# A new written-out order for the opening of a one-core attention and MLP kernel, with nine more constant matmuls and some evictions on other engines

## The chip, the cores and the metric

The kernel runs on one core of a Trainium2 chip. The metric is the device time in microseconds (us), the median of several runs; a profiled execution of the same program gives the trace. A core has five engines that run side by side: TensorE (PE in the profile; its weight loads are PEld), VectorE (DVE), ScalarE (ACT), GpSimd (POOL) and SyncE (SP). In this kernel SP issues all DMA transfers, from one queue.

## The reference

All inputs are float32; x is 1 x 2048 x 512.

```
xn = layernorm(x)                                # over the 512 columns, no affine part
qkv = xn @ wqkv                                  # 32 heads of 16
logits[s, w] = q[s] . k[s - 2w] / 4   for w = 0..7   (masked where s - 2w < 0)
s  = (softmax(logits) applied to v[s - 2w]) @ wo
y  = layernorm(xn)
h  = gelu(y @ w1 + b1)                           # 512 -> 1376
g  = silu(h @ w2 + b2)                           # 1376 -> 512
out = x + s * g
```

## The kernel before

**Numbers.** Every large matmul is done in three float16 passes: each float32 operand is split into a high half (rounded) and a low half (what the rounding left), and TensorE adds high x high, low x high and high x low in PSUM. So every activation tile and every weight block has two steps of preparation, "hi" (a scaled copy or a cast) and "lo" (a subtraction), and each is given to an engine by a table of constants at the top of the file.

**Tiles.** The sequence is split in even and odd positions (c = 0 and 1), 1024 rows each, 8 tiles of 128 rows. The heads are taken in 4 head blocks of 8 heads; a head block's weight is 512 x 384 (q, k and v). There are 8 units of attention (c, head block). Each unit has a projection on TensorE (12 matmuls of 384 columns a tile, L864), evictions of PSUM into the buffer U with a row scale (L878 on VectorE, L882 on ScalarE), halo copies of k and v by DMA (L896), products and sums on VectorE (L930, L933, L988) and GpSimd (L999, L1010), a split of the result (L971 ScalarE, L973 VectorE) and its transposition by DMA (L976). The MLP runs beside it on TensorE in 4 chunks of 4 tiles (L1143 first matrix, L1186 second). At the end the output projection is done for c = 1 (L1088), with the last head block's part in separate matmuls that come "late", after the last transposition.

**The opening.** SP loads, in an order given by the constant `LOADS` and by `ORDER` below: tiles of x as they are ("x"), two tiles already transposed on the host ("t", tiles 6 and 7), halves of the first two head blocks' weights ("q": q 0 is k = 0, 1 of the first block, q 2 is k = 2, 3; q 4 and q 6 are the second block), the four parts of the MLP's first matrix ("w"), a bias ("b"). Then:

- Tiles 6 and 7 go a direct way: their mean over columns is formed (tile 6: L685 on VectorE and a small matmul L691; tile 7: four matmuls L682), subtracted (L693, VectorE), and they are multiplied in float32 with the unscaled head block (L700, four steps a tile, step k needs quarter k of the head block).
- The first head block is scaled: squares summed on ScalarE (L597), added up over partitions by tiny matmuls (L513), a power of two worked out on VectorE (L524 to L542), then four "hi" copies on ScalarE (L619) and four "lo" steps, two on VectorE (L626) and two on GpSimd (L553, L554).
- Every x tile has statistics on VectorE (L659, L660, L714), a power on GpSimd (L718), a normalisation (L748 GpSimd, L744 ScalarE, L751 VectorE, by `Y_ENG`), and is transposed: tiles 0 to 3 by TensorE (L766), followed by a cast "hi" (L770 ScalarE or L772 VectorE, by `HI_ENG`) and a subtraction "lo" (L773); tiles 4 to 7 by a cast, a subtraction and a DMA (L756 to L758).
- The projection of the first two head blocks is issued in groups of four matmuls, so that the first four can start as soon as "hi" of a tile and of the weights are there.
- `WAKE` constant matmuls (L1305; 128 x 128 by 256 columns of constants, result unused) are issued on TensorE around the first steps.

**What sets the order.** The kernel first builds a list of operations (`Plan.add`): each has an engine, what it reads and writes, and a number in the order in which it was added. `Plan.issue` then emits them. `ORDER` (L73) lists all numbers, so the order of every engine's queue, SP's too, is written out and nothing is chosen at build time; costs and priorities in the code no longer matter. Buffers of a ring are handed out in that order too. Each engine works through its queue in order; between engines there are semaphores. An operation that is not ready therefore holds up all that stand behind it on its engine.

Of the kernel before, what the change touches and what calls it, by code (L numbers as in the profile page):

```python
# [10 lines left out]
BF16 = mybir.dt.bfloat16  # L11
# [7 lines left out]
P = 128  # L19
S, D, F = 2048, 512, 1376  # L20
H, DH, W, DIL = 32, 16, 8, 2
KT = D // P
# [10 lines left out]
LASTP = 256  # L33
# [19 lines left out]
HI_ENG = ('act', 'act', 'act', 'dve', 'dve', 'dve', 'dve', 'act')  # L53
XT = (0, 4, 30, 34)
# [7 lines left out]
EV0 = ('act', 'dve', 'dve', 'act', 'act', 'act', 'dve', 'dve')  # L62
EV1 = ('dve', 'dve', 'act', 'act', 'act', 'act', 'dve', 'act')
# [5 lines left out]
W2LATE = 6  # L69

# [287 lines left out]
PW1 = 0.423  # L358
PB1 = 0.75
PCS = 0.6  # L360
PQ0 = 0.2677
PSQ0 = 0.1788
PMEAN = 0.04
PDIR = (0.192, 0.1517, 0.1187, 0.1556)
# [1162 lines left out]
```

## Time and profile before

| | us |
|---|---|
| median of 3 runs | 412.66 |
| lowest, highest run | 412.56, 412.87 |
| span of the profiled execution | 411.0 |
| TensorE busy | 402.8 |
| VectorE busy | 381.6 |
| ScalarE busy | 224.9 |
| GpSimd busy | 132.7 |

The span is from the first to the last instruction of one execution; the run's time has something more around it. A row of a timeline has the start, the duration, the engine, the line of the program, the operation with its output and input and how many instructions were merged (x16), and in brackets how long the engine was idle before and what ended that. Consecutive rows can overlap a little, because an instruction's end is drawn with its pipeline. A float32 matmul of L682, L691 and L700 is recorded as two instructions.

### The profile page before, as it was taken

The numbers are of one execution on the slowest core, as the hardware profiler recorded it, in microseconds if no ns is written. First come the engines' busy times: TensorE is split into PE (matmuls) and PEld (weight loads), VectorE is DVE, ScalarE is ACT, GpSimd is POOL, SyncE is SP. The second block draws the span as 40 slices with busy tenths as digits, with TensorE's granted clock in tenths as the row PEclk, the third lists the DMA queues.
The fourth block names the chain that finished last, engine by engine and source line by source line (L and its number), as shares of the span: only waits on it lengthen the run. The fifth ranks groups of instructions, "written<-read, shape, count | busy, mean of one in ns | idle before, by whom it ended". The sixth has DMA issues, their size and how long they took to land.

```text
span 411.0 us, 5490 instructions
## 1 busy us (share of the span) xinstructions
PE 402.8 (98%) x2030; PEld 198.7 (48%) x2030; DVE 381.6 (93%) x386; ACT 224.9 (55%) x372; POOL 132.7 (32%) x141
## 2 busy tenths in 40 slices
PE   7899999999999999999999999999999999999996
PEld 4565544444444455445544554444445544444443
DVE  4899999999999999999889999899999989989985
ACT  3899987983989736633564164214523177236310
POOL 2843000053562425143424243233322505250012
PEclk9999999999999999999999999999999999999999
DMA  8957538251018372911251009610344452004984
GB/s 288 395 104 227 177 90 214 92 179 27 1 30 189 85 130 77 150 49 27 51 141 27 0 2 213 209 50 22 107 122 120 107 135 60 0 1 116 285 214 162
DMA packets 52627, 48.04 MB, mean 117 GB/s; under 512 B 37066, under 2 KB 37510, under 8 KB 52088
## 3 DMA queue, kind: packets, MB, share of 16 engines
q1 hardware_dynamic: 52600, 47.69, 42.8%
q8 instruction: 16, 0.26, 0.3%
q14 instruction: 11, 0.09, 0.1%
HBM read 24.40 MB, written 7.34 MB: 77 GB/s over the span
## 4 chain that ended last, share of the span: by engine, by line
PE 90%; DVE 3%; ACT 3%; DMA 1%; POOL 1%; issue 0%; SPq 0%; POOLq 0%; ACTq 0%; DVEq 0%
PE ps L864 27%; PE z L1186 25%; PE ps L1143 25%; PE ps L1056 5%; PE z L1088 2%; PE ps L1088 2%; PE z L1174 2%; DMA prod<-in_A_x_dram 1%; DVE bn L659 1%; ACT w L565 1%; ACT w L504 1%; PE pl L1088 1%; PE z L1177 1%; PE pl L864 1%; POOL prod L748 1%; DVE yT L773 0%
## 5 line engine op out<-in xcount | busy, mean ns | idle before, releaser
L864 PE MATMUL ps<-wq,yT 128*128 128x384 f16 (+1 forms) x708 | 128.9, 337 | 0.2
L1186 PE MATMUL z<-w,h 128*128 128x512 f16 x480 | 111.4, 379 | 0.0
L1143 PE MATMUL ps<-yT,w 128*128 128x512 f16 x480 | 109.0, 379 | 0.0
L864 PEld LDWEIGHTS <-yT 128*128 128x128 f16 x744 | 72.2, 98 | 59.1 <-issue 1.3
L930 DVE TENSOR_TENSOR prod<-U 128x2048 f32<-128x2048 f32 x32 | 73.8, 2312 | 4.1 <-ACT U L882 3.0
L1143 PEld LDWEIGHTS <-w 128*128 128x128 f16 x480 | 46.8, 98 | 55.6 <-issue 0.5
L933 DVE TENSOR_REDUCE L<-prod 128x128 f32<-128x2048 f32 x32 | 73.0, 2282 | 0.5
L1186 PEld LDWEIGHTS <-h 128*128 128x128 f16 x480 | 46.5, 98 | 54.6 <-issue 0.7
L999 POOL TENSOR_TENSOR prod<-prod,prod 128x1024 f32<-128x1024 f32 x14 | 41.3, 2968 | 81.3 <-DVE prod L988 81.3
L882 ACT ACTIVATE U<-ps,cs 128x384 f32<-128x384 f32 x54 | 30.1, 575 | 62.9 <-PE ps L864 62.7
L988 DVE TENSOR_TENSOR prod<-pl,U 128x2048 f32<-128x2048 f32 x28 | 63.5, 2283 | 0.3
L1156 ACT ACTIVATE ps<-ps,b1T,hsc 128x512 f32<-128x512 f32 x40 | 29.8, 747 | 37.0 <-PE ps L1143 36.8
L1159 ACT ACTIVATE h<-ps,hsc 128x512 f16<-128x512 f32 x40 | 27.4, 684 | 20.6 <-PE z L1186 19.7
L1009 POOL COPY gate<-prod 1x1 f32<-1x1 f32 x21 | 4.6, 219 | 102.2 <-DVE prod L930 102.2
L1010 POOL TENSOR_TENSOR prod<-prod 128x1024 f32<-128x1024 f32 x14 | 32.9, 2348 | 0.0
L1161 DVE SCALAR_TENSOR_TENSOR h<-ps,hsc,h 128x512 f16<-128x512 f32 x40 | 29.5, 744 | 3.2 <-ACT h L1159 3.2
L1056 PE MATMUL ps<-wo,oT 128*128 128x512 f16 x96 | 21.5, 379 | 0.0
L983 DVE TENSOR_TENSOR prod<-prod,prod 128x2048 f32<-128x2048 f32 x9 | 20.6, 2288 | 0.2
L971 ACT ACTIVATE o<-prod,osc 128x1024 f16<-128x1024 f32 (+1 forms) x9 | 9.5, 1051 | 18.0 <-DVE prod L983 9.9
L1010 POOL TENSOR_TENSOR prod<-prod,prod 128x1024 f32<-128x1024 f32 x7 | 16.4, 2347 | 0.0
L1088 PEld LDWEIGHTS <-oT 128*128 128x128 f16 x108 | 10.5, 98 | 10.4 <-issue 0.2
L1056 PEld LDWEIGHTS <-oT 128*128 128x128 f16 x96 | 9.4, 98 | 11.1
(201 smaller groups left out, 393.6 us busy)
## 6 DMA issues: line engine op xcount, KB each, us to landing
f<-in_A_x_dram SPq DMA_DIRECT2D x31, 256.0 KB, 3.1
U<-U SPq DMA_DIRECT2D x16, 392.0 KB, 6.7
gd<-f SPq DMA_DIRECT2D x12, 256.0 KB, 2.7
prod<-in_A_x_dram SPq DMA_DIRECT2D x8, 256.0 KB, 5.7
oT<-in_B_w_dram SPq DMA_DIRECT2D x2, 1024.0 KB
yT<-in_B_w_dram SPq DMA_DIRECT2D x2, 1024.0 KB
f<-gd SPq DMA_DIRECT2D x8, 256.0 KB, 5.4
out_dram<-f SPq DMA_DIRECT2D x8, 256.0 KB
```

Source lines behind the costliest of these rows:

```text
L864: nc.tensor.matmul(b.t[:, 0:wide], y[:, s, k, o:o + P], wq[hb][:, t, k], start=(n == 0), stop=(n == 11))
L882: act(384, lambda i=i, b=b: nc.scalar.activation(U3[:, i:i + 31:15, :], b.t[:, 0:384].rearrange("p (t e) -> p t e", t=3), AF.Identity, sca ...
L930: dve(2048, lambda p2=p2, g=g: nc.vector.tensor_tensor(p2(), q, slots(Ut, KH, 2 * g), op=ALU.mult), qk + [("kh", ub, 0), ("kh", ub, 1), (" ...
L933: dve(2048, lambda pr=pr, g=g: nc.vector.tensor_reduce(L3()[:, 2 * g:2 * g + 2], pr.t.rearrange("p (r f d) -> p r f d", r=2, d=DH), AX.X, ...
L988: dve(2048, lambda: nc.vector.tensor_tensor(pr.t.rearrange("p (r f d) -> p r f d", r=2, d=DH), A3()[:, 2 * g:2 * g + 2].rearrange("p r (f ...
L999: pool(2.4, lambda n=n: nc.gpsimd.tensor_tensor(acc.t[:, n:n + 1024], acc.t[:, n:n + 1024], p1.t[:, n:n + 1024], op=ALU.add), [acc, p1], [ ...
L1010: nc.gpsimd.tensor_tensor(x.t[:, 0:1024], x.t[:, 0:1024], y(), op=ALU.add)
L1056: nc.tensor.matmul(b.t, oT[:, hb, i // 4, s, i % 4], wo[:, t, hb], start=(hb == 0 and n == 0), stop=(hb == last and n == 2))
L1088: nc.tensor.matmul(b.t[:, cols], oT[:, hb, i // 4, s, i % 4], wo[:, t, hb, cols], start=(start and hb == 0 and n == 0), stop=(stop and hb ...
L1143: nc.tensor.matmul(b.t[0:M], w1[:, s, f * 512 + k * M:f * 512 + (k + 1) * M], yT[ch][:, t, k], start=(n == 0), stop=(n == 11))
L1156: act(512, lambda: nc.scalar.activation(b.t[0:M], b.t[0:M], AF.Gelu_apprx_tanh, bias=b1T[0:M, f:f + 1], scale=hsc[0:M, 1:2]), [b, ("b1T",) ...
L1186: nc.tensor.matmul(z.t, hl[s][:, t * P:(t + 1) * P], w2[:, w, f], start=(f == 0 and n == 0), stop=False)
```

## The change

Three things change what is emitted; the rest of the diff adds choices that are all set to what the kernel did before (`SUBS`, `ST_ENG`, `YLO`, `SECS`, `QH0`, `QH1`, `LASTC`, more entries in `XT` and `PDIR`, a new branch of `MEANBY`) or costs that only a planner without `ORDER` would read.

**Engines.** In the first head block's evictions, tiles 1 and 2 go from VectorE to ScalarE and tiles 3 and 4 the other way; in the second's, tiles 0 and 6 go to ScalarE and tile 2 to VectorE. The cast of tile 3 goes to ScalarE. The "hi" of the weight piece W1P[5] (1024 columns) goes from ScalarE to VectorE.

**Constant matmuls.** 28 instead of 19. The first 19 stand ahead of tile 6's mean matmul (before: 16), 4 behind it, and 5 are strewn over the queue: behind tile 7's mean, behind tile 0's transposes, two behind the second group of projections of tile 0 and one behind the last of the second block's totals.

**ORDER.** It is a new list, 1273 numbers instead of 1264, and nearly all queues differ from beginning to end. What the first operations are, queue by queue:

| queue | before | after |
|---|---|---|
| SP | t6, q0, q2, x2, x0, q4, t7, x5, x1, x3, x4, q6, w0, w2, x7, w3, x6, w1, b | t6, q2, q0, x0, t7, x2, x1, q4, x4, x5, x3, q6, w3, w2, w1, x7, x6, b, w0 |
| TensorE (without constants) | mean 6, direct 6 k=0, 1, two totals, k=2, mean 7, k=3, total, transposes 0, direct 7 (four), transposes 1, total, projection 0 (4, 4), transposes 3, projection 1 (4), 3 (4, 4, 4), ... | mean 6, direct 6 k=0, two totals, k=1, mean 7, k=2, direct 7 k=0, 1, transposes 0, direct 6 k=3, direct 7 k=2, projection 0 (4), total, direct 7 k=3, projection 0 (4), total, transposes 3, 1, 2, projection 3 (4), 1 (4), 3 (4), 1 (4, 4), 3 (4), ... |
| VectorE | mean 6, subtract 6, statistics 2, 0, scale of block 0, statistics 5, subtract 7, statistics 1, lo of weights, lo of tile 0, statistics 4, 3, ... | mean 6, subtract 6, statistics 0, scale of block 0, statistics 2, subtract 7, statistics 1, 4, 5, 3, lo of tile 0, ..., normalise 3, 2, lo of weights, scale of block 1, lo of weights, lo of tiles 3, 1, ... |
| ScalarE | squares q0, q2, q4, four hi of weights, cast 0, squares q6, normalise 1, ... | squares q2, q0, three hi of weights, squares q4, cast 0, fourth hi, squares q6, normalise 1, normalise 4, cast 3, cast 1, ... |
| GpSimd | power 0, normalise 0, power (1, 2), lo of weights, power (3, 4, 5), power of second variance, lo of weights, normalise 5, ... | power 0, normalise 0, lo of weights, power (1, 2), power (3, 4, 5), power of second variance, lo of weights, ..., normalise 5 |

Further on: VectorE's eviction of the second head block's tile 2 stands behind evictions and casts and ahead of weight halves and the first attention product (L930), and at the end two steps of the output (L1120, L1127) stand ahead of the last split (L973), which came before them.

The core of the diff:

```
-HI_ENG = ('act', 'act', 'act', 'dve', 'dve', 'dve', 'dve', 'act')
+HI_ENG = ('act', 'act', 'act', 'act', 'dve', 'dve', 'dve', 'act')
-W1ENG = ('act', 'dve', 'act', 'act', 'act', 'act', 'act')
+W1ENG = ('act', 'dve', 'act', 'act', 'act', 'dve', 'act')
-EV0 = ('act', 'dve', 'dve', 'act', 'act', 'act', 'dve', 'dve')
-EV1 = ('dve', 'dve', 'act', 'act', 'act', 'act', 'dve', 'act')
+EV0 = ('act', 'act', 'act', 'dve', 'dve', 'act', 'dve', 'dve')
+EV1 = ('act', 'dve', 'dve', 'act', 'act', 'act', 'act', 'act')
 ORDER = (
-    0, 1, 235, 19, 2, 3, 4, 5, 6, 7, 8, 9, 10, 11, 110, 111, 112, 113, 114, 115, 116, 117, 118, 119, 120, 121,
-    122, 123, 124, 125, 20, 126, 127, 128, 21, 32, 33, 163, 22, 23, 34, 54, 37, 12, 109, 108, 38, 40, 49, 35,
...
+    110, 244, 0, 109, 2, 1, 111, 112, 113, 108, 4, 114, 6, 115, 116, 117, 118, 119, 120, 121, 122, 33, 123, 124,
+    125, 3, 129, 8, 19, 134, 131, 20, 130, 32, 127, 128, 21, 135, 22, 37, 38, 34, 35, 40, 23, 36, 54, 5, 26, 49,
...
-WAKE = 19
+WAKE = 28
```

More of the change, by code (lines that the diff above doesn't have):

```diff
@@ L32 @@
 NFB = 7
-LASTP = 256
+LASTC = (0, 256, 512)
 LASTPOOL = (0, 2, 4)
@@ L69 @@
 W2LATE = 6
+SUBS = ()
+ST_ENG = ('dve',) * 8
+YLO = ('dve',) * 8
+SECS = BATCHES
+QH0 = ('act', 'act', 'act', 'act')
+QH1 = ('act', 'act')
 BEFORE_W1 = (0, 1, 4, 5)
 ORDER = (
[62 rows of a table removed]
[62 rows of a table added]
 )
@@ L671, in tile_mixer, with parts, xcs @@
     xt = {i: U[1][:, XT[n] * P:(XT[n] + 4) * P].rearrange("p (k t) -> p k t", k=KT) for n, i in enumerate(FP)}
+    def parts(i):
+        return ((0, 1), (1, KT)) if i in SUBS else ((0, KT),)
+    def xcs(i):
+        return [("xc", i, k0) for k0, k1 in parts(i)]
     def center(i):
@@ L706, in tile_mixer, with stats_act @@
     gof = {i: g for g in GROUPS for i in g}
+    def stats_act(i):
+        q, (x, xkey) = cpos[i], xk[i]
+        sm = R_s.new()
+        o, dst = (i % 4) * P, yT[i // 4]
+        junk = dst[:, 0, :, o:o + P].bitcast(BF16)
+        act(512, lambda: nc.scalar.activation(x(), x(), AF.Identity, accum_out=sm.t[:, 0:1]), [xkey], [xkey, (sm, 0)], aps=2)
+        act(1, lambda: nc.scalar.activation(mv0[:, q, 0:1], sm.t[:, 0:1], AF.Identity, scale=1.0 / D), [(sm, 0)], [("mv0", i)])
+        act(1, lambda: nc.scalar.activation(sm.t[:, 1:2], sm.t[:, 0:1], AF.Identity, scale=-D ** -1.5), [(sm, 0)], [(sm, 1)])
+        act(512, lambda: nc.scalar.activation(
+            junk, x().rearrange("p (k t) -> p k t", k=KT), AF.Square, bias=sm.t[:, 1:2], scale=D ** -0.5,
+            accum_out=mv0[:, q, 1:2]), [xkey, (sm, 1), ("mv0", i)], [("mv0", i), ("yh", 0, i)], aps=3)
     def ln0(g):
@@ L851, in qkv @@
         cp = lambda i: cpos[i] if c == 0 else i
-        raw = pl.users([("xc", j) for j in FP]) if u == 1 else set()
+        raw = pl.users([x for j in FP for x in xcs(j)]) if u == 1 else set()
         wide = 384 + FL * (hb == HLAST)
@@ L1090, in mm @@
             return go
-        parts = [(i, slice(0, D)) for i in range(NI - 1)] + [(NI - 1, slice(0, LASTP)), (NI - 1, slice(LASTP, D))]
+        parts = [(i, slice(0, D)) for i in range(NI - 1)] + [(NI - 1, slice(a, b)) for a, b in zip(LASTC, LASTC[1:])]
         banks = {}
@@ L1291, in tile_mixer @@
                     y0(i)
-    for n, g in enumerate(BATCHES):
+    for n, g in enumerate(SECS):
         with prio(PSEC[n]):
```

43 lines of the change are left out of this document (31 added, 12 removed), and 120 rows, old and new, of the table ORDER.

## The prediction

> **What bounds the kernel now.** I read the page first, then a table of stretches, then the timelines of the opening and of the end.
>
> ```profile
> span 411.0 us, 5490 instructions
> PE 402.8 (98%) x2030; PEld 198.7 (48%) x2030; DVE 381.6 (93%) x386; ACT 224.9 (55%) x372; POOL 132.7 (32%) x141
> PE 90%; DVE 3%; ACT 3%; DMA 1%; POOL 1%; issue 0%; SPq 0%; POOLq 0%; ACTq 0%; DVEq 0%
> ```
>
> TensorE is busy 98% and carries 90% of the chain that ended last; VectorE with 93% stands close behind it. The table of stretches says where TensorE's missing share lies (in each row, the second figure is TensorE's busy time, the fourth VectorE's):
>
> ```profile
> 0.00:5.00 5.00, 3.81 (x17) 2.70 (x18) 1.51 (x5) 1.74 (x2) 2.59 (x11) 1.00 0.64 209
> 5.00:10.00 5.00, 3.42 (x13) 1.64 (x12) 2.75 (x9) 2.00 (x5) 0.19 (x1) 1.00 1.02 360
> 10.00:15.00 5.00, 4.20 (x21) 2.93 (x22) 4.25 (x12) 4.04 (x11) 4.06 (x4) 1.00 1.03 408
> 15.00:20.00 5.00, 4.42 (x26) 2.37 (x25) 4.45 (x18) 4.22 (x7) 4.39 (x6) 1.00 1.03 405
> 20.00:60.00 40.00, 39.87 (x228) 21.81 (x226) 38.21 (x64) 37.30 (x67) 8.29 (x6) 1.00 0.54 145
> 60.00:300.00 240.00, 239.91 (x1200) 116.15 (x1199) 229.71 (x198) 134.76 (x231) 86.96 (x86) 1.00 0.37 91
> 300.00:396.00 96.00, 96.00 (x475) 45.56 (x474) 90.79 (x70) 40.52 (x55) 22.06 (x28) 1.00 0.43 114
> 396.00:411.00 15.00, 11.17 (x60) 5.57 (x57) 9.91 (x16) 0.32 (x1) 4.18 (x3) 1.00 0.55 176
> ```
>
> In the first 20 us TensorE idles 1.19 + 1.58 + 0.80 + 0.58 = 4.15 us. From 20 to 396 it idles 0.13 + 0.09 + 0 = 0.22 us in all. So the time is: when TensorE gets going, plus a fixed amount of matmul, plus the tail. Only the opening has time to give, and an order that is worse later can only take. The opening as TensorE lives it:
>
> ```profile
> 1.19 3.57 PE L1305 MATMUL z<-first,fours 128*128 128x256 bf16 x16 [1.19 <-DVE first L440]
> 4.64 0.79 PE L691 MATMUL ps<-f,first 128*128 128x128 f32 x2
> 6.21 1.56 PE L700 MATMUL pl<-prod,U 128*128 128x384 f32 x4 [0.27 <-DVE U L693]
> 10.12 1.16 PE L682 MATMUL ps<-U,first 128*128 128x128 f32 x8 [1.14 <-DMA U<-in_A_xt_dram]
> 12.61 0.66 PE L766 MATMUL z<-first,prod 128*128 128x128 f32 x4 [0.69 <-POOL prod L748]
> 13.11 2.75 PE L700 MATMUL z<-prod,U 128*128 128x384 f32 x8
> 16.33 1.46 PE L864 MATMUL ps<-wq,yT 128*128 128x384 f16 x8
> 18.24 0.66 PE L766 MATMUL z<-first,prod 128*128 128x128 f32 x4 [0.45 <-DVE ssq L524]
> 18.73 5.84 PE L864 MATMUL ps<-wq,yT 128*128 128x384 f16 x32
> 19.68 4.57 PE L864 MATMUL ps<-wq,yT 128*128 128x384 f16 x26
> ```
>
> Constant matmuls fill up to 4.64; then come the mean and direct projection of tile 6 (L691, L700), the same for tile 7 (L682, L700), the transposes of the first normalised tiles (L766) and the first projections (L864). The last row, from an answer that begins at 19.6, marks where tile 3's projection starts; from there on TensorE is practically full. That instant is my milestone.
>
> What these steps wait for are the loads:
>
> ```profile
> 2.12 0.91 SPq L1233 DMA_DIRECT2D prod<-in_A_x_dram  x2
> 3.56 1.03 DVE L685 TENSOR_REDUCE f<-U 128x128 f32<-128x512 f32 x1 [2.05 <-DMA U<-in_A_xt_dram]
> 4.54 0.84 ACT L597 ACTIVATE wq<-prod 128x768 bf16<-128x768 f32 x1 [2.53 <-DMA prod<-in_A_wqkv_dram]
> 7.08 0.84 ACT L597 ACTIVATE wq<-prod 128x768 bf16<-128x768 f32 x1 [1.60 <-DMA prod<-in_A_wqkv_dram]
> 7.76 0.69 DVE L659 BATCH_NORM_STATS2 bn<-prod 128x6 f32<-128x512 f32 x1 [1.60 <-DMA prod<-in_A_x_dram]
> 8.59 0.66 DVE L659 BATCH_NORM_STATS2 bn<-prod 128x6 f32<-128x512 f32 x1
> 10.49 2.07 POOL L748 TENSOR_SCALAR prod<-prod,mv,rb 128x512 f32<-128x512 f32 x1
> ```
>
> The loads of places 1 to 4 in SP's queue land at 3.56, 4.54, 7.08 and 7.76 (a waiting engine starts then), and place 7, tile 7 transposed, at 10.12.
>
> **The change, part by part.**
>
> *Loads.* Places 1 to 7 become: tile 6, second half of the head block, first half, x tile 0, tile 7, x tile 2, x tile 1. The sizes of places 1 to 4 stay (256, 384, 384, 256 KB), so I give them the same landings. Place 5 is estimated at 7.76 + 0.68 = 8.44, with the step from place 3 to 4. So tile 7 comes 1.7 us earlier. Tile 0's statistics start at 7.76 instead of 8.59 because its load is first and VectorE no longer takes tile 2 ahead of it. The price: the half with k = 0 and 1, which the direct projection of tile 6 needs first, lands at 7.08 instead of 4.54. SP issues about every 0.46 us (0.91 for two), the same number as before, so the queue itself costs nothing.
>
> The Trainium skill (DMA: Bandwidth & Descriptors, on queues, rings and completion order) speaks against landing by place: a ring takes descriptors up in order, but transfers need not complete in the order in which they were issued. Every landing seen here is in order, yet places 2 and 3, of one size, are 2.54 us apart, which a strict one-after-the-other would not give. If only the address of the late half counted and not its place, the direct projection would start about 0.6 us earlier than in my sum.
>
> *TensorE's walk to the milestone.* 19 constants instead of 16 stand ahead of tile 6's mean: (4.64 - 1.19) / 16 = 0.216 each, 1.19 + 19 x 0.216 = 5.29. Its sum is ready at 3.56 + 1.03 = 4.59, so the three more delay it by 0.65; that is hidden, because the mean (0.79) and four constants end before 7.08 and the first direct step waits for its half until then. A step takes 0.65 to 0.7 (2.75 us hold four, each recorded as two). The two totals wait for ScalarE: 7.08 + 0.84 and an accumulator read, 8.1. Second step to 8.8; tile 7's mean (landed 8.44; 1.16 less the tail that the next covers) to 9.8; a constant and a third step to 10.6; VectorE's subtraction (0.7, behind tile 2's statistics) ends at 10.85; two steps of tile 7 to 12.15. Tile 0 by then: 1.90 from the start of its statistics to GpSimd's normalisation (8.59 to 10.49), so 9.66, plus 2.07: 11.7. Its transposes need not wait at 12.15; they take 0.5 (12.61 to 13.11), a constant 0.1. A step each of tiles 6 and 7 to 14.05, first four projections (0.7: 4.57 / 26 each) to 14.75, last step to 15.4, second four to 16.1, three constants and a total to 16.5, three tiles' transposes to 18.0. Tile 3's projection begins at 18.0, against 19.68.
>
> Of the nine added constants four stand ahead of 7.08, where TensorE waits anyway; the other five stand behind 9.7. Their cost there is not in the trace: above it is 0.216 each by the early row, below it 0.12, two thirds of the 5.84 / 32 = 0.18 of a late 384-column matmul. I take 0.12 because they come as late as that row: 0.6 together, in the walk already; at 0.216 the walk is 0.5 longer. The Trainium skill (TensorE: Matmul & The Clock Gate, Part 1) says that the array runs at half clock until it has been busy some 3.4 us and falls back after as long an idle window; by its full-clock rate such a constant costs 0.107, the five 0.53, and the sum would be 0.07 better. The page's clock column reads 1.00 throughout; the spacing of the rows agrees with the rule.
>
> At the milestone the new order lacks one group of four projections (0.7) and has one tile's transposes more (0.5). Gain of the opening: 19.68 - 18.0 - 0.2 = 1.5, less 0.1 for a wait on VectorE's low half of tile 3 right behind: **1.4 us**. Bounds: 0.3 if the direct steps and GpSimd slip together by the 1.1 us that TensorE waits at 10.12 now; 2.0 with the earlier half.
>
> *GpSimd and ScalarE queues.* GpSimd's low half of the first weights now runs before the power of tiles 1 and 2; behind it queue those powers, and behind them ScalarE's tile 1 and VectorE's tile 2. GpSimd is free at 11.7 instead of 12.56, and the half, a scaling and a subtraction of 384 columns, is bounded by the 2.07 of the row above, so the power is at worst a microsecond late, and at best in time. Tiles 1 and 2 are transposed last in the walk, near 17, which covers it. The scale of the MLP's first matrix now waits for its first quarter, the last load; the bytes are the same, so it lands when the old last one did.
>
> *Engines of evictions and halves.*
>
> ```profile
> L882 ACT ACTIVATE U<-ps,cs 128x384 f32<-128x384 f32 x6 | 3.3, 572 | 0.1
> L878 DVE TENSOR_SCALAR U<-ps,cs 128x384 f32<-128x384 f32 x5 | 3.0, 609 | 0.4 <-PE ps L864 0.4
> L770 ACT CAST yT<-z 128x512 f16<-128x512 f32 x3 | 1.7, 583 | 1.7 <-PE z L766 0.9 <-PE ps L513 0.7
> L772 DVE CAST yT<-z 128x512 f16<-128x512 f32 x1 | 0.7, 691 | 0.2 <-PE z L766 0.2
> L565 ACT ACTIVATE w<-o,hsc 128x1024 f16<-128x1024 f32 x1 | 1.1, 1132 | 0.0
> L563 DVE TENSOR_SCALAR w<-oT,hsc 128x512 f16<-128x512 f32 x1 | 0.5, 486 | 0.0
> ```
>
> Four evictions go to ScalarE and three to VectorE, one cast goes to ScalarE, one weight half of 1024 columns to VectorE. VectorE: -4 x 0.61 + 3 x 0.61 - 0.69 + 2 x 0.49 = -0.32 us. ScalarE: 0.57 + 0.58 - 1.13 = 0. Small, but an eviction on VectorE stands in its order and waits for its matmuls: the second block's tile 2 behind TensorE's group, with weight halves and the first attention product queued behind it.
>
> *The rest of the order.* Nearly every queue is reordered to the end.
>
> ```profile
> DVE prod L930 <- ACT U L882: 3.0, 2, 1.5
> ```
>
> This is VectorE waiting for a new head block before its first attention product: twice, up to 1.5 us. The trace cannot show the new order. It can gain at most the 0.22 us that TensorE idles from 20 to 396; what it costs has for its nearest row that same 0.22 and, far off, one such VectorE wait passed on whole. I take a cost of 0.3, near the first.
>
> *The tail caps it.*
>
> ```profile
> 395.78 0.75 DVE L973 SCALAR_TENSOR_TENSOR o<-prod,osc,o 128x512 f16<-128x512 f32 x1 [0.79 <-ACT o L971]
> 396.78 1.24 SPq L976 DMA_TRANSPOSE oT<-o  x1
> 399.54 6.32 PE L1088 MATMUL z<-wo,oT 128*128 128x512 f16 x30
> yT<-f SPq DMA_TRANSPOSE x12, 3.6
> ```
>
> The last attention half leaves VectorE at 396.53 and is transposed by a DMA issued at 396.78; with 3.6 us to landing it is there at 400.4. TensorE needs it behind nine more matmuls from 399.54 (0.216 each): 401.5. So TensorE has 1.1 us to spare; running further ahead it waits. That slack moves with VectorE: its 0.32 less work adds, but two steps of the output now precede that last split and fill its 0.79 wait with about 1.4, which takes 0.65. Slack 0.8 to 1.4; I take 1.0.
>
> **Sum**, against the profiled execution: gain 1.4 - 0.3 = 1.1 at the last stage, of which 1.0 passes the tail: span 411.0 - 1.0 = 410.0. The median of the runs is 412.66, 1.66 above that span, for what lies around it; I keep this: **411.7 us**.
>
> **The rivals.**
>
> *VectorE becomes the bound (slower).* VectorE idles only 1.8 us from 20 to 60. If its eviction of tile 2 waits there for TensorE and one later block comes late, each by the 1.5 of that row, less the 0.8 by which tile 0 starts earlier, it is 2.2 late at the last split. It decides beyond the 1.0 of slack: +1.2, 413.9. For it: 93% busy, and the added evictions sit in its queue. Against: its load falls.
>
> *The whole gain reaches the end.* VectorE gains in the opening as well, the tail moves along and nothing is given back: 1.4 to 2.0, so 411.3 to 410.7, about 410.9. Against: VectorE's end is set by its own 381.6 us.
>
> *Nothing measurable.* The walk slips to its bound of 0.3 and the later 0.3 eats it: 412.7.
>
> **How the numbers follow.** Forecast 0.45 (its own range 411.2 to 412.3), slower rival 0.23 (413.2 to 414.7), whole gain 0.13, nothing 0.19. A change under 0.2%, 0.83 us, cannot be told here. Of the forecast's case 0.29 lies below 411.83 and 0.16 above: faster 0.29 + 0.13 = 0.42, same 0.16 + 0.19 = 0.35, slower 0.23. The range from 410.8 to 413.9 leaves out half of the slower rival and half of the whole gain.
>
> **What would show it.** Tile 0's statistics at 7.8, tile 7's mean before 9, first projection at 14.05, tile 3's at 18.0; TensorE's idle in the first 20 us down to about 2.5; no wait over 0.4 us on TensorE from 20 to 396; the last split near 396 and TensorE waiting up to half a microsecond for the transposed half. Wrong if tile 3's projection starts after 19, or if VectorE's last split comes after 397.

## The result, and the profile after

The changed kernel takes 416.57 us (median of 4 runs, 416.01 to 417.43); the kernel before took 412.74 beside it (412.56 to 412.87). The ratio is 1.0100, with a 95% interval from 1.0086 to 1.0114. It is slower by 1%, where the prediction had it faster by 0.2%.

The page of the changed kernel, with the same three lines as before (span; busy time of the engines; the chain that ended last):

```profile
span 414.2 us, 5506 instructions
PE 403.9 (98%) x2039; PEld 199.5 (48%) x2039; DVE 382.5 (92%) x385; ACT 229.0 (55%) x377; POOL 133.5 (32%) x141
PE 57%; DVE 24%; ACT 10%; issue 6%; DMA 2%; POOL 1%; SPq 0%; DVEq 0%; ACTq 0%
```

TensorE carries 57% of the chain now, and VectorE and ScalarE a third of it. ScalarE is busy 4.1 us longer. In the table of stretches (second figure TensorE's busy time, fourth VectorE's) the opening is better and everything behind it is worse:

```profile
0.00:5.00 5.00, 3.81 (x19) 2.72 (x20) 1.52 (x5) 1.77 (x2) 2.58 (x11) 1.00 0.64 214
5.00:10.00 5.00, 4.74 (x26) 3.06 (x24) 3.82 (x12) 3.07 (x8) 2.13 (x2) 1.00 1.02 369
10.00:15.00 5.00, 5.00 (x23) 3.04 (x24) 4.72 (x18) 3.79 (x8) 3.63 (x6) 1.00 1.05 412
15.00:20.00 5.00, 5.00 (x38) 3.54 (x37) 4.90 (x13) 4.86 (x9) 3.22 (x3) 1.00 1.04 414
20.00:60.00 40.00, 39.17 (x219) 21.00 (x217) 34.37 (x58) 36.61 (x68) 9.19 (x7) 1.00 0.60 167
60.00:300.00 240.00, 236.48 (x1181) 113.94 (x1179) 229.76 (x198) 133.19 (x226) 82.99 (x84) 1.00 0.33 86
300.00:396.00 96.00, 95.38 (x467) 44.80 (x466) 90.91 (x68) 43.82 (x58) 25.98 (x28) 1.00 0.40 106
```

TensorE idles 1.45 us in the first 20 us (before: 4.15). The work that it still has to do at 20 us is 403.9 - 18.55 = 385.4 now, and was 402.8 - 15.85 = 386.95: in these two profiles the opening put it 1.6 us ahead. From 20 to 396 us it then idles 0.83 + 3.52 + 0.62 = 4.97 us, where it idled 0.22. That is 4.75 lost against 1.6 won, and 1.6 - 4.75 is the difference of the spans, 411.0 against 414.2. VectorE idles 5.63 us from 20 to 60 (before 1.79).

Three things in the trace could be behind the 4.75 us. The first is ScalarE's function tables. The groups of ScalarE have rows for the loads; before:

```profile
L1156 ACT ACT_TABLE_LOAD x10 | 12.8, 1283 | 1.3 <-PE ps L1143 1.1
L956 ACT ACT_TABLE_LOAD x8 | 10.3, 1283 | 0.1
L1202 ACT ACT_TABLE_LOAD x3 | 3.8, 1283 | 0.1
```

and after (L999 is the exponential of the softmax, L1199 Gelu, L1245 Silu):

```profile
L1199 ACT ACT_TABLE_LOAD x13 | 16.7, 1283 | 9.4 <-PE ps L1186 9.2
L999 ACT ACT_TABLE_LOAD x8 | 10.3, 1283 | 6.3 <-DVE L L997 6.2
L1245 ACT ACT_TABLE_LOAD x5 | 6.4, 1283 | 0.1
```

With those of other lines there are 28 loads instead of 24. More telling is the last figure: ScalarE stood idle 0.1 us ahead of the exponentials' loads, since other work was queued; now it waits 6.3 us for VectorE's subtraction L997, and only then loads. VectorE in turn waits for the result before it can form the sums (L1001), with too little queued in between. From 200 to 396 us (the time in all, how often, the longest), before and after:

```profile
DVE mx L958 <- ACT L L956: 0.6, 1, 0.6
```

```profile
DVE mx L1001 <- ACT L L999: 4.6, 3, 2.0
```

The second is what stands behind such an exponential in ScalarE's queue. At 288 us of the changed kernel:

```profile
288.01 1.28 ACT L999 ACT_TABLE_LOAD   x1 [1.78 <-DVE L L997]
289.30 0.63 ACT L999 ACTIVATE L<-L 128x512 f32<-128x512 f32 x1
290.06 0.33 ACT L929 ACTIVATE hl<-ps,hsc 128x96 f32<-128x96 f32 x1
290.44 1.78 PE L907 MATMUL ps<-wq,yT 128*128 128x480 f16 x8 [0.87 <-ACT hl L929]
```

The eviction L929 stands behind the exponential, and TensorE needs its PSUM. The Trainium skill (ScalarE: Activation LUTs, What ACT_TABLE_LOAD costs) gives 1283 ns for a load, which these rows show, and some 1380 ns of draining beside it, which they do not: the exponential starts 0.01 us after its load ends, and ahead of the eight loads of the kernel before ScalarE idled 0.1 us in all.

The third is in a group of VectorE. The product L973 (L930 before) is one shape, and took 2312 ns on average and 73.8 us in all:

```profile
L973 DVE TENSOR_TENSOR prod<-U 128x2048 f32<-128x2048 f32 x32 | 77.0, 2412 | 1.6 <-DMA U<-U 0.2
```

The 3.2 us more are two single products, here with what ran beside them:

```profile
171.06 6.71 POOL L1042 TENSOR_TENSOR prod<-prod,prod 128x1024 f32<-128x1024 f32 x2 [10.25 <-DVE prod L1031]
171.12 4.43 DVE L973 TENSOR_TENSOR prod<-U 128x2048 f32<-128x2048 f32 x1 [0.21 <-DMA U<-U]
176.27 1.04 PE L1229 MATMUL z<-w,h 128*128 128x512 f16 x4 [1.60 <-DVE h L1204]
...
343.29 6.71 POOL L1042 TENSOR_TENSOR prod<-prod,prod 128x1024 f32<-128x1024 f32 x2 [14.20 <-DVE prod L1031]
343.72 4.06 DVE L973 TENSOR_TENSOR prod<-U 128x2048 f32<-128x2048 f32 x1
```

Each begins just after GpSimd has begun an addition, and lasts 4.43 and 4.06 us instead of 2.29, as if it did nothing until the first of the two additions was over. That addition takes 2.35 us, and the second 4.40, until 2.2 us after the product has ended: each waits for the other in turn. TensorE waits 1.60 us behind the first, for a half (L1204) that VectorE has queued after it.

### The profile page after: what moved, and what is told of

Same layout as the page of the kernel before. It is cut to its first block, busy times and chain, and to the rows that moved or that the text cites. A ratio compares the mean times of both kernels' runs of the same rounds, so it can differ in the third digit from the quotient of the medians.

```text
span 414.2 us, 5506 instructions
## 1 busy us (share of the span) xinstructions
PE 403.9 (98%) x2039; PEld 199.5 (48%) x2039; DVE 382.5 (92%) x385; ACT 229.0 (55%) x377; POOL 133.5 (32%) x141
## 4 chain that ended last, share of the span: by engine, by line
PE 57%; DVE 24%; ACT 10%; issue 6%; DMA 2%; POOL 1%; SPq 0%; DVEq 0%; ACTq 0%
PE ps L907 18%; PE z L1229 13%; PE ps L1186 12%; DVE L L976 5%; DVE prod L1031 5%; PE ps L1099 4%; DVE prod L973 3%; PE z L1131 2%; DVE h L1204 2%; DVE w L575 2%; PE ps L1131 2%; DMA U<-U 2%; ACT L999 1%; PE pl L907 1%; PE z L1217 1%
## 5 line engine op out<-in xcount | busy, mean ns | idle before, releaser
L973 DVE TENSOR_TENSOR prod<-U 128x2048 f32<-128x2048 f32 x32 | 77.0, 2412 | 1.6 <-DMA U<-U 0.2
L925 ACT ACTIVATE U<-ps,cs 128x384 f32<-128x384 f32 x56 | 31.7, 576 | 60.9 <-PE ps L907 51.8
L1031 DVE TENSOR_TENSOR prod<-pl,U 128x2048 f32<-128x2048 f32 x28 | 63.2, 2284 | 1.6 <-POOL prod L1042 1.3
L1042 POOL TENSOR_TENSOR prod<-prod,prod 128x1024 f32<-128x1024 f32 x14 | 39.2, 2824 | 73.1 <-DVE prod L1031 42.2
L1199 ACT ACTIVATE ps<-ps,b1T,hsc 128x512 f32<-128x512 f32 x40 | 29.5, 747 | 29.9 <-PE ps L1186 29.7
L1204 DVE SCALAR_TENSOR_TENSOR h<-ps,hsc,h 128x512 f16<-128x512 f32 x40 | 29.6, 744 | 4.6 <-ACT h L1202 4.6
L1199 ACT ACT_TABLE_LOAD x13 | 16.7, 1283 | 9.4 <-PE ps L1186 9.2
L1053 POOL TENSOR_TENSOR prod<-prod,prod 128x1024 f32<-128x1024 f32 x7 | 16.4, 2347 | 0.0
L1131 PEld LDWEIGHTS <-oT 128*128 128x128 f16 x108 | 10.3, 98 | 10.5 <-issue 0.5
```

The lines of the kernel that those rows point to most:

```text
L925: act(384, lambda i=i, b=b: nc.scalar.activation(U3[:, i:i + 31:15, :], b.t[:, 0:384].rearrange("p (t e) -> p t e", t=3), AF.Identity, sca ...
L973: dve(2048, lambda p2=p2, g=g: nc.vector.tensor_tensor(p2(), q, slots(Ut, KH, 2 * g), op=ALU.mult), qk + [("kh", ub, 0), ("kh", ub, 1), (" ...
L1031: dve(2048, lambda: nc.vector.tensor_tensor(pr.t.rearrange("p (r f d) -> p r f d", r=2, d=DH), A3()[:, 2 * g:2 * g + 2].rearrange("p r (f ...
L1042: pool(2.4, lambda n=n: nc.gpsimd.tensor_tensor(acc.t[:, n:n + 1024], acc.t[:, n:n + 1024], p1.t[:, n:n + 1024], op=ALU.add), [acc, p1], [ ...
L1053: nc.gpsimd.tensor_tensor(x.t[:, 0:1024], x.t[:, 0:1024], y(), op=ALU.add)
L1199: act(512, lambda: nc.scalar.activation(b.t[0:M], b.t[0:M], AF.Gelu_apprx_tanh, bias=b1T[0:M, f:f + 1], scale=hsc[0:M, 1:2]), [b, ("b1T",) ...
```

## Experiments

Two theories at the start. **A**: the loss lies in the new order behind 60 us, through the table loads. **B**: it lies between 20 and 60 us, where VectorE idles 3.84 us more and starts the attention no earlier than before. Later A split into **A1** (the four added loads), **A2** (the loads of the exponentials), **A3** (what stands behind a waiting exponential), and **A4** came in (VectorE and GpSimd shut each other out). In kernels whose `ORDER` was replaced, lines are two further down than in the changed kernel. The 18 runs, beside the kernel before on the same chip; "more" is the difference of the medians:

| run | median | more | ratio, 95% interval |
|---|---|---|---|
| changed kernel | 416.57 | 3.83 | 1.0086 to 1.0114 |
| e1 new to 60 us, then old | 412.29 | 0.28 | 0.9994 to 1.0015 |
| e2 old to 60 us, then new | 422.02 | 10.01 | 1.0203 to 1.0312 |
| e3 new, one table | 412.91 | 0.90 | 1.0008 to 1.0037 |
| e4 old, one table | 412.58 | 0.57 | 1.0000 to 1.0019 |
| e5 new, Silu as Gelu | 414.88 | 2.50 | 1.0050 to 1.0102 |
| e6 new, Gelu as Exp | 413.17 | 0.79 | 1.0005 to 1.0029 |
| e7 new to 200 us, then old | 412.13 | -0.25 | 0.9983 to 1.0007 |
| e8 new, three moves | 415.27 | 3.13 | 1.0044 to 1.0099 |
| e9 new, six moves | 416.19 | 4.05 | 1.0080 to 1.0107 |
| e10 as e7, 19 constants | 412.47 | 0.33 | 1.0005 to 1.0038 |
| e11 searched order | 419.51 | 7.37 | 1.0163 to 1.0191 |
| e12 new, short additions | 414.28 | 1.98 | 1.0030 to 1.0061 |
| e13 old, short additions | 412.14 | -0.16 | 0.9985 to 1.0003 |
| e14 new to 30 us, then old | 412.18 | -0.12 | 0.9984 to 1.0005 |
| e15 as e14, searched 15 to 48 us | 412.18 | -0.12 | 0.9982 to 1.0000 |
| e16 new, one table, short additions | 410.34 | -2.22 | 0.9916 to 0.9955 |
| e17 new, eight moves | 414.73 | 2.17 | 1.0044 to 1.0081 |
| e18 new order, old engines | 419.19 | 6.63 | 1.0148 to 1.0189 |

**Where: two hybrids at 60 us.** The first takes the operations that start before 60 us in the changed kernel, and their engines, and then the old order; the second is the complement.

```
-ORDER = (the changed kernel's 1273)
+ORDER = (its 301 that start before 60 us, then the other 972 as they stood before)
```

> Every operation that starts before 60 us in the changed kernel stands in its new place and on its new engine, with all 28 constants; the rest stands in the order of the kernel before. Theory A (the loss lies in the new order behind 60 us, where ScalarE loads function tables 28 times instead of 24, 1.283 us each, in places where VectorE and TensorE wait for it): 411.1 to 412.8, the 1.6 us of the opening kept in part. Theory B (VectorE's idle time from 20 to 60, 5.63 us against 1.79, starts the attention no earlier than before and VectorE carries that to the end): 415.5 to 416.6, the whole loss is in this kernel.

```
-ORDER = (the changed kernel's 1273)
+ORDER = (the 285 that start before 60 us in the kernel before, then the rest as in the changed kernel)
-WAKE = 28
+WAKE = 19
```

> The complement: what starts before 60 us in the kernel before keeps its order and its engines, with 19 constants; the rest stands in the new order. Theory A: 416 to 418, all of the loss and none of the opening's 1.6 us. Theory B: 412.3 to 413.2, level with the kernel before.

The first is level with the kernel before: the new loads, engines, constants and everything to 60 us, taken together, cost nothing. B falls as the cause of the loss. The opening's gain is spent, though: in the profile of this hybrid TensorE idles 1.40 us from 20 to 396 us, where the kernel before idled 0.22. VectorE gains nothing either: the first attention product starts at 43.42 us before and at 43.76 in the changed kernel, behind two waits that the new order made. Before, and after:

```profile
43.42 2.28 DVE L930 TENSOR_TENSOR prod<-U 128x2048 f32<-128x2048 f32 x1
```

```profile
34.39 0.62 DVE L921 TENSOR_SCALAR U<-ps,cs 128x384 f32<-128x384 f32 x1 [1.97 <-PE ps L907]
...
43.10 0.75 DVE L1204 SCALAR_TENSOR_TENSOR h<-ps,hsc,h 128x512 f16<-128x512 f32 x1 [1.59 <-ACT h L1202]
43.76 2.28 DVE L973 TENSOR_TENSOR prod<-U 128x2048 f32<-128x2048 f32 x1
```

That start differs between executions: it lies at 42.37, 42.88 and 43.42 us in three profiles of the old order (e13, e2, before), at 43.05 to 45.48 in twelve of the new one.

The second is worse than A said, by 4 us. A new fault is in it: the new order behind 60 us counts on steps that the old one does later, and at the seam TensorE waits 2.8 us in one place and VectorE 4.3 in another. So it says only that the new rest is bad, not how bad.

**The loads: one table.** In both kernels:

```
-AF.Gelu_apprx_tanh
+AF.Exp
-AF.Silu
+AF.Exp
```

> The changed kernel with Gelu and Silu replaced by Exp, so that ScalarE needs one function table for the whole kernel (other values come out, the same instructions run). If the table loads are the cause (theory A), VectorE's waits for the exponential (4.7 us in all, row of L1001) shrink to about 1, and the time falls to 411 to 413. If they are not (theory B), 415 to 416.6, less at most the 1 us by which every chain through ScalarE gets shorter.

> The kernel before with the same replacement, the base for the changed kernel with one table. TensorE idles 0.22 us from 20 to 396 us there, so table loads can hold up little: 411.7 to 412.8 by both theories. Theory A has the changed kernel with one table within 1 us of this one, or below it; theory B has it 2.5 to 4 above.

Theory A holds: without the loads 2.9 of the 3.8 us are gone, while the old order gains nothing (0.57 above itself). The 24 loads of the old order were free; the 28 of the new one were not.

**Which loads.** In the changed kernel:

```
-AF.Silu
+AF.Gelu_apprx_tanh
```

> The changed kernel with Silu replaced by Gelu (other values, the same instructions): no load for the Silu steps, so the four loads that the new order adds (before 213.7, 215.8, 345.9 and 348.7 us) are gone, and the eight pairs around the exponentials stay. Theory A1 (the four added loads cost the time): 0.5 to 1.2 us above the kernel before. Theory A2 (the loads in front of the exponentials cost it, because VectorE has nothing left to do between L997 and L1001 at 205, 288 and 332 us): 2.5 to 3.8 above.

```
-AF.Gelu_apprx_tanh
+AF.Exp
```

> The changed kernel with Gelu replaced by Exp: no loads around the exponentials, and the loads around the Silu steps stay, the added four among them. Theory A1: 2.5 to 3.8 us above the kernel before. Theory A2: 0.5 to 1.2 above. If both are 1.5 to 2.5 above, the two kinds share the loss.

A2 rather than A1. Without Silu ten loads are gone, the four added ones among them, and 2.5 us remain, with 18 loads where 24 cost the old order nothing. Without Gelu 12 loads are left, none of them around the exponentials, and 0.8 us remain. It is not the number of loads that costs, but their place: VectorE waits 4.6 us for three of the eight exponentials in the first kernel, as in the changed one, and 1.4 us for two in the second. What the four added loads cost stays open, since the four executions without Silu spread from 413.39 to 416.50.

**Where again: a hybrid at 200 us.**

```
-ORDER = (the changed kernel's 1273)
+ORDER = (its 740 that start before 200 us, then the other 533 as they stood before)
```

> As the first hybrid, with the border at 200 us instead of 60: the new order to 200 us, the old one behind it. TensorE's idle time between 60 and 200 us in the changed kernel is 2.36 us, 1.6 of it in one wait near 176 us behind a halo copy by DMA and a product that takes 4.43 us instead of 2.29. If these count, 1.5 to 2.5 us above the first hybrid, so 1.8 to 2.8 above the kernel before. If the loss lies with the loads behind 200 us (exponentials at 205, 288 and 332 us, the four added ones), level with the first hybrid, at most 0.8 above the kernel before.

Level with the kernel before. Behind 200 us TensorE idles nothing up to 396 in this profile (1.77 us in the changed kernel's), since the old order is back there. But from 60 to 200 us, too, it idles only 0.70 us (2.37 in the changed kernel's): the one long wait, behind the product at 171 us, is absent here, with the same steps in the same order:

```profile
170.48 2.29 DVE L975 TENSOR_TENSOR prod<-U 128x2048 f32<-128x2048 f32 x1
170.66 6.62 POOL L1044 TENSOR_TENSOR prod<-prod,prod 128x1024 f32<-128x1024 f32 x2 [10.24 <-DVE prod L1033]
```

VectorE was first this time and took its 2.29 us; GpSimd's two additions took 6.62 together. So the loss does not lie behind 200 us alone; what is lost at 171 us is lost in some executions and not in others.

**Mending the order, with the loads in mind.** Numbers are those of the changed kernel's `ORDER`.

```
-951 (L929) behind 1004 (L999)      +951 ahead of 998 (L1014)
-779 (L1245) ahead of 775 (L1202)   +779 behind 775
-785 (L1245) ahead of 840 (L1202)   +785 behind 840
```

> The changed kernel with three steps moved on ScalarE behind 200 us, the number of table loads unchanged: the eviction that TensorE waited for at 290 us (L929, behind the exponential of 289.3) goes ahead of L1014 at 284.6; the Silu step at 210.3 goes behind the half L1202 at 210.9; the Silu step at 217.1 goes behind the half L1202 at 218.2. Theory A3 (an exponential waits for VectorE's L997 and then for its table load, and what stands behind it in ScalarE's queue holds up TensorE): 1 to 2 us less than the changed kernel, so 1.8 to 2.8 above the kernel before. If only the number of loads counts: 3.4 to 4.2 above, as the changed kernel.

```
 the three moves, and
-1003 (L997) behind 915, 916        +1003 ahead of 915 (L1113)
-1158 (L997) behind 1182, 977       +1158 ahead of 1182 (L1204)
-1247 (L1170) ahead of 1177         +1247 behind 1177 (L1016)
```

> The same with three moves on VectorE: the subtraction L997 ahead of two output steps at 285.9, ahead of a half L1204 at 374.6, so that the exponential behind it starts earlier, and one output step (L1170) at the end behind the last split L1016. Theory A3: 0.8 to 2.0 us above the kernel before, at least 0.5 less than with the three moves alone. If VectorE's queue does not matter: as with the three moves.

A3 is not borne out. By the medians three moves gave 0.7 us, within a spread from 412.9 to 416.9, and three more, on the very subtractions that the exponentials wait for, gave nothing. Either profile shows two stretched products (4.4 us at 253 and 4.07 at 343), which may hide what the moves gave.

**The constants.**

```
-WAKE = 28
+WAKE = 19
```

> The hybrid with its border at 200 us without the nine added constants. Of them five stand where TensorE does not wait for anything else, 0.108 us each: 0.4 to 0.6 less than that hybrid, so 0.5 to 1.0 below the kernel before. If the constants are needed there (for TensorE's clock) or lie in TensorE's waits: level with that hybrid or above it.

No gain: 0.33 above the kernel before, against 0.25 below with them. In its profiled execution the product of 173 us met an addition (3.99 us), in that of e7 it did not; that alone is more than the 0.5 us in question. Its executions spread from 411.91 to 415.45, and the profiled one is the slowest. So the nine constants are not what slows the kernel, and whether the five of them that stand behind 9.7 us cost half a microsecond, as forecast, stays open.

**A searched order.** The order behind the opening was rearranged by adding up the traces' durations, each table load included, along the queues.

```
-ORDER = (the changed kernel's 1273)
-WAKE = 28
+ORDER = (the list of e1, single steps behind 15 us moved)
+WAKE = 24
```

> The new engines, the new opening and 24 constants; behind the opening an order found by moving single steps as long as the end comes earlier when the durations of the traces, 1.283 us for each table load among them, are added up along the queues. That sum puts it 3 us below the first hybrid. If order alone was the loss, and with table loads in the sum it can be foreseen: 1 to 3 us below the kernel before. If the sum misses something as large as the loads were: level or above.

7.4 us slower: the sum with the loads alone misses much more. VectorE is busy 386.5 us in it, though its work is the same, and some of its instructions are stretched beside GpSimd's, as at 171 us. But most of TensorE's idle time lies ahead of 60 us, 6.4 of 7.9 us up to 396 (the changed kernel idles 2.3 there), and the first attention product waits for a halo copy:

```profile
DVE prod L975 <- DMA U<-U: 3.1, 1, 3.1
```

The product starts at 48.71 us, 4.3 later than in the first hybrid. The granted clock, too, was 0.96 from 60 to 100 us in this profile.

**The additions: A4.** The additions of the first two products on GpSimd, in both kernels:

```
-nc.gpsimd.tensor_tensor(acc.t[:, n:n + 1024], acc.t[:, n:n + 1024], p1.t[:, n:n + 1024],
+nc.gpsimd.tensor_tensor(acc.t[:, n:n + 64], acc.t[:, n:n + 64], p1.t[:, n:n + 64],
```

> The changed kernel with GpSimd's additions of L1042 cut from 1024 to 64 columns (most of the sum over the first two products is left out), so that they no longer run beside a VectorE product of L973. Theory A4 (a VectorE instruction on two operands in SBUF and a GpSimd addition shut each other out, and the new order makes them meet): the stretched 2.1 and 1.7 us and a wait of 1.3 for GpSimd go, 1.5 to 3 us less than the changed kernel, so 0.8 to 2.3 above the kernel before. If the loads alone cost the time: 3.4 to 4.2 above.

> The kernel before with the same cut. Its products are stretched by 0.84 us once. Theory A4: 0 to 0.8 us less than the kernel before, so that the two orders come within 0.8 to 2 us of each other. If the additions hold up both orders alike: as much less as the changed kernel loses.

A4 holds: 1.85 of the 3.83 us go from the new order and 0.16 from the old, which leaves them 2.1 us apart, just beyond the 2 expected. The products are all of one length again:

```profile
L973 DVE TENSOR_TENSOR prod<-U 128x2048 f32<-128x2048 f32 x32 | 73.2, 2293 | 1.7 <-DMA U<-U 0.5
```

This rule stands in the Trainium skill (SBUF — State Buffer, Who interferes with whom): a VectorE instruction with two inputs in SBUF and a GpSimd instruction that reads SBUF do not share, and the one that comes second is blocked until the first has ended. The rows agree (2.29 became 4.43); products that take one input from PSUM (L1031) kept their 2284 ns on average in the changed kernel, though eight of the 28 ran beside an addition.

**Both together.** The replacements of the one-table kernel and the short additions:

```
-AF.Gelu_apprx_tanh, AF.Silu; acc.t[:, n:n + 1024]
+AF.Exp, AF.Exp; acc.t[:, n:n + 64]
```

> The changed kernel with Gelu and Silu replaced by Exp and the additions of L1042 cut to 64 columns, so with neither table loads nor long additions there. If loads and additions are the whole loss: 0.5 below to 0.4 above the kernel before, no further from it than with one table alone. If a third cause remains: 0.6 to 1.5 above.

2.2 us below the kernel before, where level was expected: without the two causes nothing of the loss remains. TensorE is full behind 60 us again:

```profile
60.00:200.00 140.00, 139.83 (x700) 67.49 (x699) 136.05 (x130) 83.31 (x159) 37.41 (x53) 1.00 0.37 89
200.00:300.00 100.00, 100.00 (x503) 48.57 (x501) 94.96 (x72) 31.73 (x55) 22.84 (x32) 1.00 0.30 82
300.00:396.00 96.00, 96.00 (x474) 45.49 (x473) 90.60 (x71) 30.89 (x47) 18.08 (x27) 1.00 0.43 117
```

Alone they take 2.9 and 1.85 us away, together 6.05. The opening's gain may explain part of what lies below the kernel before; that is not shown. The old order with both was not run; with either alone it gains nothing, and its TensorE has 0.22 us of idle time from 20 to 396 us to give.

**Mending the order, with both in mind.**

```
 951 (L929) ahead of 960             1158 (L997) ahead of 1182
 1117 (L1031) behind 1052 (L1204)    1041 (L1245) behind 1051 (L1202)
 771 (L1229) behind 838              1247 (L1170) behind 1177
 968 (L861) ahead of 1016            977 (L870) ahead of 1147
```

> The changed kernel with eight steps moved behind 200 us, this time with both the table loads and the exclusion of VectorE and GpSimd in the sum: the eviction L929 of 290.1 us further ahead, the subtraction L997 of 375.6 and the half L870 of 375.2 ahead of a half and a product, the product L1031 of 338.7 two places later (away from GpSimd's addition), the Silu step of 340.1 behind the half of 340.7, nine matmuls of L1229 at 205.7 later, the activation L861 of 304.2 earlier, an output step L1170 at the end later. If the two causes are what binds: 3 to 4 us less than the changed kernel, 0.3 below to 0.8 above the kernel before. If the sum still misses something: 2 or more above.

1.7 of the 3.8 us are gone, where the sum had 3 to 4. The product of 343 us is not stretched any more, but the one of 171 us still is, and one at 255 us, in the profile of the slowest of five executions. The rows show by how little:

```profile
172.00 4.42 DVE L975 TENSOR_TENSOR prod<-U 128x2048 f32<-128x2048 f32 x1 [0.23 <-DMA U<-U]
...
255.46 6.71 POOL L1044 TENSOR_TENSOR prod<-prod,prod 128x1024 f32<-128x1024 f32 x2 [10.71 <-DVE prod L1033]
255.51 4.44 DVE L975 TENSOR_TENSOR prod<-U 128x2048 f32<-128x2048 f32 x1 [0.20 <-DMA U<-U]
```

The same two in the profile of the changed kernel:

```profile
255.00 2.29 DVE L973 TENSOR_TENSOR prod<-U 128x2048 f32<-128x2048 f32 x1
255.04 4.48 POOL L1042 TENSOR_TENSOR prod<-prod,prod 128x1024 f32<-128x1024 f32 x1 [10.49 <-DVE prod L1031]
```

There VectorE was first by some 40 ns, here GpSimd by 50. The product waits for a halo copy (the bracket), GpSimd for the end of another product, and the two come at nearly the same instant: if VectorE comes second it loses 2.15 us. No sum of durations foresees that. At 171 us GpSimd came first in four (the changed kernel, e3, e10, e17) of nine profiles that have the new order up to there, VectorE in five (e5 to e9). At 343 us it is no race: where the new order and the long additions stand there, GpSimd is first by 0.43 us or more in every profile. And in five profiles with the old order there (before, e1, e13, e14, e15) VectorE is first by 0.22 to 0.23 us at both products, of 172 and 252 us.

**The opening's gain at the end.**

```
-ORDER = (the changed kernel's 1273)
+ORDER = (its 178 that start before 30 us, then the other 1095 as they stood before)
```

> The hybrid with its border at 30 us: the new opening, and from 30 us on the old order, the second block's tile 2 back on ScalarE among the rest. If VectorE's two waits at 34.4 and 43.1 us (1.97 and 1.59) ate the opening's gain, the first attention product starts some 0.7 us before 43.4 and the end follows it: 0.4 to 1.0 below the kernel before. If the gain is lost elsewhere: level with it, as the hybrids at 60 and 200.

```
-ORDER = (the list of e14)
-WAKE = 28
+ORDER = (the same, steps between 15 and 48 us moved, DMA issues excepted)
```

> The hybrid at 30 us with the steps between 15 and 48 us moved, DMA issues excepted, until VectorE's first attention product comes earliest by the durations of the traces, table loads and the exclusion between VectorE and GpSimd in the sum; behind 48 us the order of the kernel before. The sum puts that product 2.2 us before that hybrid's, 40.5 us. If the end follows the first product: 1.5 to 3 below the kernel before. If the sum misses something in this stretch, as in the first searched order: level or above.

Both are level with the kernel before. The first attention product starts 0.8 us earlier than in the profile of the kernel before in e14, as forecast, and 0.5 in e15, where the sum had 2.9; what it waits for now is a halo copy:

```profile
42.58 2.29 DVE L975 TENSOR_TENSOR prod<-U 128x2048 f32<-128x2048 f32 x1 [0.61 <-DMA U<-U]
```

```profile
42.88 2.29 DVE L975 TENSOR_TENSOR prod<-U 128x2048 f32<-128x2048 f32 x1 [1.14 <-DMA U<-U]
```

(e14 and e15.) The old order itself has that product at 42.37 us in e13, so neither start shows a gain. TensorE, for its part, idles 1.06 us from 20 to 60 us in e14 (0.13 before). And the last split stands at 394.34 us in e14 (395.78 before), but at the end TensorE then waits for the transposing DMA:

```profile
401.06 4.39 PE L1133 MATMUL z<-wo,oT 128*128 128x512 f16 x21 [0.86 <-DMA oT<-o]
```

The profiled span of e14 is 410.6, that of e15 409.9, against 411.0; in the medians nothing of it is left beyond 0.12 us. No version that does the whole computation beats the kernel before by more than can be measured.

**The engines alone.**

```
-HI_ENG, W1ENG, EV0, EV1 of the changed kernel
+HI_ENG, W1ENG, EV0, EV1 of the kernel before
```

> The changed kernel with the engine tables of the kernel before (evictions, cast and weight half back). They touch only steps before 60 us, where the first hybrid showed no loss: 3.0 to 4.8 above the kernel before. If the new engines cost the time: 1.5 above or less.

2.8 us slower than the changed kernel, beyond the range: the new engines help the new order. With the old ones VectorE starts the attention at 45.66 us in the profile, later than in any of the twelve with the new ones, and three products are stretched.

## Why the prediction was wrong

*The opening* went as described, and faster in this execution. The estimate of the landings was late: the half with k = 0 and 1 is there when ScalarE takes it up at 5.57 us (7.08 forecast), so that the first direct step waits for VectorE's subtraction and not for a load. VectorE begins tile 0's statistics at 6.50 us (7.76 forecast), tile 7's mean is formed from 8.14, the first projection starts at 13.21 (14.05) and tile 3's at 16.93 (18.0).

```profile
5.57 0.84 ACT L603 ACTIVATE wq<-prod 128x768 bf16<-128x768 f32 x1
6.50 0.69 DVE L673 BATCH_NORM_STATS2 bn<-prod 128x6 f32<-128x512 f32 x1
6.61 0.91 PE L725 MATMUL pl<-prod,U 128*128 128x384 f32 x2 [0.24 <-DVE U L717]
13.21 0.81 PE L907 MATMUL ps<-wq,yT 128*128 128x384 f16 x4
16.93 0.81 PE L907 MATMUL ps<-wq,yT 128*128 128x384 f16 x4
```

The forecast gain of 1.4 us is 1.6 in TensorE's remaining work, but the landings are one draw, before and after. ScalarE takes up the second half between 5.57 and 7.44 us in the 16 profiles that begin with the new loads, between 6.03 and 7.08 in three that begin with the old ones. TensorE's busy time in the first 20 us is 15.85, 16.29 and 16.50 us in those three (before, e13, e2), and 17.28 to 18.68 in eleven with the new opening whole, 18.37 in the middle one. Less the 1.1 us of more constants, the gain is about 1.0 us in the middle, and the 1.6 had some luck in it.

*The constants* were sized rightly: a late one takes 0.11 us from its start to the next matmul's (9.03 to 9.14), and TensorE is busy 403.9 - 402.8 = 1.1 us longer for nine.

*The rest of the order* is the step that failed: "it can gain at most the 0.22 us that TensorE idles from 20 to 396; what it costs has for its nearest row that same 0.22 ... I take a cost of 0.3, near the first". It cost 4.75 us of idle TensorE. The row was the wrong one: how little an order idles says how well that order was fitted, not what another would cost. Two rows of the kernel before said what a misfit could cost, and neither stands in the prediction. The loads of function tables (21 in the three groups above, 1.283 us each) were hidden there, ScalarE being idle 0.1 us ahead of the exponentials' loads. And one product of 32 had taken 3.13 us beside a GpSimd addition; it stands in the row of that line of the kernel before (shortest, median and longest in ns, below), and with the other runs it reads as a first meeting of the two engines. Both covers were properties of the order, and the change replaced the order.

```profile
L930 DVE TENSOR_TENSOR prod<-U x32: 2277/2284/3135, 43.4 to 365.3; 128x2048 f32<-128x2048 f32 x32
```

*Engines*: VectorE's load was to fall by 0.32 us; it rose by 0.9. The two stretched products of the profiled execution hold 2.14 + 1.77 us of waiting and the one before 0.84, so the rest of its work is 2.2 us shorter; the moved evictions, cast and half make 0.5 of that. *The tail*: VectorE's last split was to stay near 396; it is at 400.71. TensorE, itself 3.2 us late, runs on without a wait for the transposed half, so the slack of the sum played no part.

```profile
400.71 0.74 DVE L1016 SCALAR_TENSOR_TENSOR o<-prod,osc,o 128x512 f16<-128x512 f32 x1
```

*The slower rival* had the right engine and even its first wait: the eviction of the second block's tile 2 waits 1.97 us for TensorE, as it described. But the first hybrid has that wait too and is level with the kernel before. The rival priced the change at 413.9 through two late blocks; what made it 416.57 were the exponentials' loads and the meetings with GpSimd.

What stays open: how much of the 6.05 us that both together give back is waiting for GpSimd's sums, which the short additions also take away; why the two together give back more than the sum of each alone; and whether the changed kernel's spread between executions comes from the races, since it was profiled once, and the race at 171 us was seen to go both ways only across kernels that share this part of the order.

## What to carry to other kernels

An order written out by hand hides fixed costs (a table load ahead of an exponential, an engine pair that excludes each other) behind work that happens to stand there; before replacing it, list those costs and what covers each, for the busy engine's idle time shows only that they are covered. An engine at 92% that depends on a chain through another engine needs something queued between its question and the answer. And where two engines exclude each other, put the second one behind an event that the first one sets, instead of leaving it to two arrivals within 50 ns (not tried here). Times of landings from a single profile are one draw; a sum that rests on them needs a second.

## What the hardware showed that was not expected

Whether VectorE or GpSimd comes first, by 40 or 50 ns, decides which of them waits: 2.29 and 4.48 us at 255 us in one kernel, 4.44 and 2.35 (the first of the pair that takes 6.71) in another. GpSimd's two additions together take 6.79 us in the first and 6.71 in the second, so coming first gains it nothing, and only VectorE's time differs. Executions of such orders also spread more: 412.9 to 416.9 with three moves and 411.9 to 415.5 in e10, while the 93 runs of the kernel before beside the experiments lay between 411.5 and 413.8.

The same transfers land at different times in different executions. ScalarE took up the two halves of the first head block 2.54 us apart in the profile of the kernel before, 1.49 and 1.60 apart in two others with the same order of loads (e13, e2), and 0.98 to 2.91 apart with the new one. So the gap of 2.54 us says nothing about the place of a load in the queue.
